# Attention and two MoE layers on one core: the MoE-only part without GpSimd, x staged by quarters, and fewer loader steps a turn

## The chip, the cores and the metric

The kernel runs on one core of a Trainium2 chip. The core has five engines with a queue of instructions each: TensorE (PE in the profile, its weight loads PEld), VectorE (DVE), ScalarE (ACT), GpSimd (POOL) and SyncE (SP, which here only issues DMAs). An engine takes its instructions strictly in the order of its queue; a semaphore makes one wait for another engine. The metric is device time in microseconds (us); lower is better.

## The reference

Attention with a threshold, then two feed-forward layers on its output:

```python
scores = scale * np.matmul(q, k.transpose(0, 1, 3, 2))        # 4 batches, 8 heads, 576 tokens, 64 wide
thresh = np.max(scores, axis=-1, keepdims=True) - tau
scores = np.where(scores >= thresh, scores, -1000000000.0)
attn = np.exp(scores - max); attn = attn / (sum + 1e-09); attn_out = np.matmul(attn, v)
x = attn_out as (2304 tokens, 512)
g = x @ w_gate; x = (g * sigmoid(g) * (x @ w_val)) @ w_out    # MoE 1: 512 -> 1536 -> 512
h = np.maximum(x @ w_in, 0.0); out = (h * h) @ w_out          # MoE 2: 512 -> 2048 -> 512
```

The weights are given in float64.

## The kernel before

Every product is made from operands that are split into a high part and a low part, three matmuls for one (high by high, high by low, low by high). So whatever TensorE reads has first to be split: a copy that gives the high part (on ScalarE, `ops.copy`, line 48) and a subtraction that gives the low part (`ops.sub`, line 56).

The program has two parts. Phase 1 (to line 850) is attention, with the first group of MoE 1 in its gaps. Phase 2 (from line 853) is MoE alone, and the change concerns it. It walks over seven groups of feed-forward tiles of 128 columns: group 0 (the last batch's share of MoE 1's first group, two blocks of 288 tokens, five tiles), groups 1 and 2 (the rest of MoE 1, three and four tiles) and groups 3 to 6 (MoE 2, four tiles each); from group 1 on a group has six blocks of 384 tokens. The names carry this: `k3_1_2_u` is group 3, block 1, tile 2.

A block is a step of `chain` (line 331). Its units come first, one for each tile: `gate_val` (two products of 12 matmuls each) or `relu2` (one product of 12). Line 218 is their matmul. What reads a product follows in stages (`mp.post`): for `relu2` ScalarE's Relu (L292), VectorE's square (L293), ScalarE's copy to the high part of `u`, VectorE's subtraction for its low part (L56, `k_u`). For `gate_val` they are a tanh (L238) and VectorE's L239 and L248, then the same copy and subtraction. The block's second product (`out1` L263, `out2` L309) reads the `u` of all its tiles. It is emitted two units into the next block (one in group 0), so those units cover the time that the last `u` takes.

Two more streams run beside this. First, x of the next block is split into `xs` (`stage_x`, line 167) in four chunks: ScalarE copies all four, GpSimd subtracts three and VectorE the fourth ("AAAA", "PPPD" on line 899). `xs` has two buffers. Second, the weights of the next group come in by pieces of 128x256 (`Loader`, line 97). A piece goes through a DMA into `wr` (L120), an absolute value on ScalarE (L129, into `wf`), four bit operations on VectorE (L131, L133, L137, L139, called the loader's first to fourth step below), a copy on ScalarE (the high part of `w`) and a subtraction on GpSimd (L56, the low part). `wr` and `wf` have three buffers, so a piece's DMA waits until the third piece before it is through L139. Lines 924 to 929 advance the loader after every three matmuls of a unit: a start, and up to one step on GpSimd, two on ScalarE and two on VectorE.

The framework sorts what was emitted by readiness and priority, so a queue need not keep the order of emission: loader steps move ahead to where their engine would be free. The queues shown below are the sorted ones.

Of the kernel before, what the change touches and what calls it, by code (L numbers as in the profile page):

```python
# [18 lines left out]
P = 128  # L19
# [16 lines left out]
# the upper word of float64 2**-127, read as a float32  # L36
# [26 lines left out]
def attention_moe(tc, qkv, qk0, tau, w1, w2, out, cfg):  # L63
# [14 lines left out]
    # MoE 1's output: the last batch's has a tile of its own, in phase 2  # L78
# [15 lines left out]
    # The weights come in as float64. A piece of a tile is brought to float32 from its bits: sign and  # L94
    # top exponent bit, the seven low exponent bits and the mantissa's first 23. What is too small for
    # float32 is raised to an exponent that gives 0 there. Then it is split.
    class Loader:
        """Brings the weights of f tiles in, piece by piece, each a little further at every call."""

        def __init__(self):  # L100
            self.bufs = []
            self.todo = []
            self.live = []
            self.n = 0
            self.age = 0

# [5 lines left out]
        def start(self):  # L112
            self.age += 1
            if not self.todo or sum(x[2] < 6 for x in self.live) >= LIVE:
                return
            src, f, w, c0 = self.todo.pop(0)
            self.n += 1
            sl = slice(c0, c0 + PIECE)
            raw, fl = self.bufs[self.n % LIVE]
            nc.sync.dma_start(raw, src[f, :, sl])  # L120
            g = self.steps(raw, fl, w[:, 0, sl], w[:, 1, sl], self.n)
            self.live.append([g, next(g), 1, "S", self.age, (f, c0)])

        def steps(self, raw, fl, whi, wlo, n):
# [17 lines left out]
            yield "P"  # L142
            ops.sub(cfg["wl"][self.n % 2], wlo, fl, whi.bitcast(F32))

        def tick(self, eng):
            """The next step on that engine, of the first piece that can take it."""
# [9 lines left out]
        def until(self, f, col):  # L156
            """Brings in what is left of tile f up to that column."""
            while any(x[1] == f and x[3] < col for x in self.todo) or any(
                x[5][0] == f and x[5][1] < col for x in self.live
            ):  # L160
                self.start()
                for e in "PADDDDP":
                    self.tick(e)
# [3 lines left out]
    def stage_x(src, xs, t0, n, eh, el):  # L167
        for c in range(NC):
# [4 lines left out]
    # split operands: hi*hi, hi*lo, lo*hi  # L173
    TERMS = [(c, a, b) for c in range(NC) for a, b in ((0, 0), (0, 1), (1, 0))]

    class Mm:
        """PSUM tiles of one bank each. What reads them is emitted in stages, later than the products."""
# [50 lines left out]
    # MoE 1, one f tile on one block: gate and value products, silu(gate) * value, split  # L228
# [100 lines left out]
    # Chains steps: a step's second product follows the next step's first unit, and what a step  # L329
    # needs first is made ready during the step before.  # L330
    def chain(steps, sync):
# [4 lines left out]
        def begin(i):  # L336
            if i < len(steps) and i not in begun:
                begun.add(i)
                steps[i]["begin"]()

        for i, s in enumerate(steps):
# [3 lines left out]
            us = []  # L345
            for j in range(s["G"]):
                u = None
                for u, c in s["unit"](j):
                    yield c
                us.append(u)  # L350
                if j == s.get("ahead", 0) and i + 1 < len(steps) and steps[i + 1].get("need") == s.get("need"):
                    begin(i + 1)
# [11 lines left out]
    # ======================= phase 1: attention, with MoE 1's first group in its gaps =======================  # L364
# [3 lines left out]
    # the last batch's part of xF is not written before the other batches are through: at first the loader has it  # L368
# [11 lines left out]
    # a column next to the scores passes every threshold and meets the 1e-9 that is added to the sum  # L380
# [5 lines left out]
    # half of the scores on either side of a bank's end  # L386
# [24 lines left out]
    def head(h):  # L411
        """The tiles of a head: queries' high and low parts one above the other, keys' twice, values' side by side."""
# [9 lines left out]
    # Where TensorE has time to spare (the first batch), products with the values may be in float32: then the  # L422
    # probabilities and the values stay whole. They lie in x2, which has nothing in it yet.
# [3 lines left out]
    def whole(p, i):  # L427
        """Is tile i of pair p (are all or some tiles of the pair) so treated?"""
# [22 lines left out]
    def first_pair():  # L451
        """Each head is loaded twice, one below the other, and split in both places."""
# [33 lines left out]
    def pair_steps(p):  # L486
        """A pair's queries and keys are split with one head above the other, then brought to their tiles by DMA."""
# [143 lines left out]
    def halves(t):  # L631
        """A tile's two PSUM tiles: the first slot of each, how many, and the way of its low parts."""
# [107 lines left out]
    def fill_group():  # L740
        """One whole product of MoE work; its PE columns, or None when there is none to do."""
# [19 lines left out]
    def work(i):  # L761
        """At most one product an iteration: attention's first, else MoE's."""
# [89 lines left out]
    # ======================= phase 2: MoE 1's other groups, then MoE 2 =======================  # L852
# [24 lines left out]
    wts[0] = W  # L877
    for _ in range(len(groups[1][2])):
        load_next(1)
# [6 lines left out]
    def steps2():  # L886
        for idx in range(len(groups)):
# [5 lines left out]
            for j, (t0, n) in enumerate(blocks):  # L893
# [3 lines left out]
                def begin(d=d, t0=t0, n=n, nm=nm, kind=kind):  # L897
                    xs = xs2.tile([P, 2, NC, n], F32R, name=f"xs_{nm}", tag="xs")
                    d["xs"] = stage_x([(0, xF)] if kind == 1 else x2, xs, t0, n, "AAAA", "PPPD")

                def end(idx=idx, j=j):
# [8 lines left out]
                    "begin": begin,  # L910
# [12 lines left out]

    for _ in chain(steps2(), mp2.drain):
        mp2.age += 1
        mp2.flush()
        loader.start()
        for e in "PADDA":
            loader.tick(e)
# [6 lines left out]
def pack(inputs):  # L936
# [37 lines left out]
# Engines: A ScalarE, D VectorE, P GpSimd. "early" and "early0" (first batch): how far ahead of its place in the  # L974
# program the scheduler may take a step.
# [13 lines left out]
    "wl": "PP",  # L989
# [36 lines left out]
```

## Time and profile before

| | |
|---|---|
| time, median of 3 runs | 1233.13 us (1233.12 to 1233.24) |
| span of the profiled execution | 1234.0 us; the page gives no other time of it |
| PE busy | 1177.9 us, 95% |
| DVE busy | 878.7 us, 71% |
| ACT busy | 654.1 us, 53% |
| POOL busy | 519.1 us, 42% |
| mean granted TensorE clock | 0.988 |

The profiled span is 0.9 us above the median. Phase 2's first matmul starts at 485.91 us, its last ends 3.8 us before the span's end; the rows below take that part apart. In a row of the timeline the first number is the start, the second how long the instruction lasted, and what stands in brackets is the idle time ahead of it and who ended it. Since instructions of one engine overlap at their ends, the time that one occupies its engine is the distance to the start of the next, where that one waits for nothing.

### The profile page before, as it was taken

How to read it: one execution, taken by the hardware profiler on the slowest of the kernel's cores; microseconds unless marked ns; L12 is line 12 of the kernel's file. 1: busy time of each engine (PE TensorE's matmuls, PEld its weight loads, DVE VectorE, ACT ScalarE, POOL GpSimd, SP SyncE). 2: the span in 40 equal slices, each digit the busy share in tenths (PEclk: the TensorE clock that was granted, in tenths of full speed). 3: DMA queues.
4: the chain of work that ended last, by engine and by line, in shares of the span. 5: the costliest groups of instructions: out<-in, count | busy, mean ns of one | idle time of the engine just before them, and what ended most of it. 6: DMA issues, size and time to landing. Idle time of an engine off the chain costs nothing.

```text
span 1234.0 us, 20272 instructions
## 1 busy us (share of the span) xinstructions
PE 1177.9 (95%) x7008; PEld 1083.3 (88%) x7008; DVE 878.7 (71%) x1911; ACT 654.1 (53%) x1622; POOL 519.1 (42%) x649
## 2 busy tenths in 40 slices
PE   5999988999999999899899999998998999899998
PEld 4655878999999999899899999997997999799997
DVE  6877997899898983979845953478349648844453
ACT  5777877888777873545323421255445434533231
POOL 4445865677666743435222321153135215421120
PEclk9999999999999999999899999998999999999999
DMA  5564453444333401323300300012002101100111
GB/s 168 146 183 122 125 136 79 102 112 115 89 89 89 117 2 35 112 77 96 93 2 26 110 2 1 1 50 88 1 6 93 40 1 50 37 1 1 52 49 54
DMA packets 40854, 84.80 MB, mean 69 GB/s; under 512 B 5936, under 2 KB 6960, under 8 KB 40752
## 3 DMA queue, kind: packets, MB, share of 16 engines
q1 hardware_dynamic: 40752, 83.52, 24.2%
q8 instruction: 55, 0.90, 0.3%
q14 instruction: 47, 0.39, 0.1%
HBM read 52.23 MB, written 4.72 MB: 46 GB/s over the span
## 4 chain that ended last, share of the span: by engine, by line
PE 69%; DVE 17%; issue 5%; ACT 3%; POOL 2%; DMA 2%; SPq 1%; DVEq 0%; POOLq 0%; ACTq 0%
PE mm L218 24%; PE mm L309 14%; PE mm L263 7%; PE s L561 5%; PE bank L218 5%; PE bank L621 5%; PE bank L263 4%; PE bank L680 3%; PE bank L677 3%; DVE wf L137 3%; DVE wf L139 2%; DVE wf L133 2%; DVE e L590 1%; DVE wf L131 1%; DVE k_u L56 1%
## 5 line engine op out<-in xcount | busy, mean ns | idle before, releaser
L218 PE MATMUL mm<-xs_k,w 128*128 128x384 f32 (+1 forms) x2400 | 413.2, 330 | 0.5 <-ACT x L48 0.5
L218 PEld LDWEIGHTS mm<-xs_k,w 128*128 128x128 f32 x2400 | 407.8, 188 | 2.5 <-ACT x L48 0.7
L309 PE MATMUL mm<-w,k_u 128*128 128x512 f32 x864 | 210.2, 400 | 13.8 <-ACT k_u L48 9.4
L309 PEld LDWEIGHTS mm<-w,k_u 128*128 128x128 f32 x864 | 165.0, 193 | 52.8 <-ACT k_u L48 11.7
L56 POOL TENSOR_TENSOR w<-wf,w 128x256 fp32r<-128x256 f32 x116 | 98.6, 858 | 180.4 <-ACT w L48 180.3
L621 PE MATMUL bank<-ident,e 128*128 128x128 f32 x720 | 163.4, 279 | 6.8 <-POOL e L601 2.7
L601 POOL TENSOR_SCALAR e<-e,r 128x576 f32<-128x576 f32 x144 | 114.2, 794 | 86.4 <-DVE r L596 37.4
L48 ACT ACTIVATE k_u<-k_th 128x384 fp32r<-128x384 f32 (+1 forms) x148 | 76.6, 518 | 137.6 <-DVE k_th L293 77.3
L56 POOL TENSOR_TENSOR xs_k<-x,xs_k 128x384 fp32r<-128x384 f32 (+1 forms) x60 | 66.5, 1128 | 181.2 <-ACT xs_k L48 180.1
L56 DVE TENSOR_TENSOR k_u<-k_th,k_u 128x384 fp32r<-128x384 f32 (+1 forms) x148 | 92.5, 625 | 68.3 <-ACT k_u L48 68.0
L218 PE MATMUL bank<-xs_m,w 128*128 128x288 f32 x720 | 136.8, 325 | 2.0 <-DVE xs_m L56 1.7
L590 DVE SCALAR_TENSOR_TENSOR e<-s,thr,e 128x577 f32<-128x577 f32 x144 | 117.0, 813 | 15.5 <-ACT thr L581 8.1
L621 PEld LDWEIGHTS bank<-ident,e 128*128 128x128 f32 x720 | 95.5, 141 | 29.4 <-issue 16.3
L573 DVE TENSOR_REDUCE nm<-s 128x1 f32<-128x576 f32 x144 | 108.4, 754 | 18.1 <-PE s L561 16.9
L263 PE MATMUL mm<-k_u,w 128*128 128x384 f32 (+1 forms) x624 | 111.1, 336 | 8.1 <-DVE k_u L56 4.3
L263 PEld LDWEIGHTS mm<-k_u,w 128*128 128x128 f32 x624 | 107.9, 195 | 9.4 <-DVE k_u L56 5.1
L579 ACT ACTIVATE e<-s,nm 128x576 f32<-128x576 f32 x144 | 107.4, 746 | 15.0 <-PE bank L621 8.5
L218 PEld LDWEIGHTS bank<-xs_m,w 128*128 128x128 f32 x720 | 111.2, 189 | 4.5 <-DVE xs_m L56 3.4
L641 ACT ACTIVATE pt<-bank 128x384 fp32r<-128x384 f32 (+1 forms) x216 | 92.0, 437 | 35.8 <-PE bank L621 31.6
L293 DVE TENSOR_TENSOR k_th<-k_th 128x384 f32<-128x384 f32 x96 | 69.0, 719 | 58.7 <-ACT k_th L292 58.6
L292 ACT ACTIVATE k_th<-mm 128x384 f32<-128x384 f32 x96 | 46.3, 483 | 112.4 <-PE mm L218 112.4
L680 PE MATMUL bank<-pt,vs 128*128 128x256 f32 (+1 forms) x480 | 93.0, 322 | 1.6 <-POOL pt L56 1.2
(92 smaller groups left out, 1846.7 us busy)
## 6 DMA issues: line engine op xcount, KB each, us to landing
wr<-in_w_dram SPq DMA_DIRECT2D x106, 256.0 KB, 3.1
raw<-in_qkv_dram SPq DMA_DIRECT2D x15, 896.0 KB, 4.8
kh<-land SPq DMA_DIRECT2D x60, 144.0 KB, 2.6
kl<-raw SPq DMA_DIRECT2D x60, 144.0 KB, 2.7
xF<-in_w_dram SPq DMA_DIRECT2D x30, 256.0 KB, 2.9
out_dram<-xF SPq DMA_DIRECT2D x18, 256.0 KB, 2.0
qs<-land SPq DMA_DIRECT2D x30, 144.0 KB, 2.4
qs<-raw SPq DMA_DIRECT2D x30, 144.0 KB, 2.6
```

The costliest lines, as they stand in the source:

```text
L48: nc.scalar.activation(out, in_, AF.Copy)
L56: e.tensor_tensor(out, a, b, op=ALU.subtract)
L218: mm(pt[:, :n], w[:, a, col + c * P : col + (c + 1) * P], xs[:, b, c, :], start=(i == 0), stop=(i == len(TERMS) - 1),)
L263: mm(pt[:, :n], w[:, a, 2 * DM + m * P : 2 * DM + (m + 1) * P], u[:, b, :], start=(k == 0), stop=(k == last),)
L309: mm(pt, u[:, b, s * P : (s + 1) * P], w[:, a, DM : 2 * DM], start=(k == 0), stop=(k == last),)
L573: nc.vector.tensor_reduce(nm, sv, axis=AX.X, op=ALU.max, negate=True)
L579: nc.scalar.activation(e[:, :S], st[t]["s"][:, :S], AF.Exp, bias=st[t]["nm"])
L590: nc.vector.scalar_tensor_tensor(e, st[t]["s"][:, : S + 1], st[t]["thr"], e, op0=ALU.is_ge, op1=ALU.mult, accum_out=sum_)
L601: nc.gpsimd.tensor_scalar(e, e, scalar1=r, scalar2=1.0, op0=ALU.mult, op1=ALU.mult)
L621: mm(dst[:, j], e[:, c0 : c0 + P], ident, is_transpose=True, start=(j == 0), stop=(j == len(cols) - 1),)
L641: nc.scalar.activation(pt[:, s0 : s0 + n, o : o + P], src, AF.Copy)
L680: mm(o[:, :n], hd["vs"][:, SLOT[k % 5], :], pt[:, k, lo : lo + n], start=(k == 0), stop=(k == 9))
```

## The change

In phase 2 the subtractions for `xs` and for the weights go from GpSimd to VectorE. `chain` begins the next block's x by quarters, one after every fourth yield of a unit (three matmuls a yield), in place of all four after the first unit. The loader starts a piece only at every second turn and only while fewer than two pieces (three before) are short of their fourth step; a turn ticks ScalarE once, VectorE once, and VectorE a second time at every fourth turn. Phase 1 keeps its settings. Lines in the changed kernel stand 14 to 15 further down (L56 and L48 stay). Comments that the change takes out are left out here.

```diff
-            if not self.todo or sum(x[2] < 6 for x in self.live) >= LIVE:
+            if not self.todo or sum(x[2] < 6 for x in self.live) >= cfg["live"][self.phase]:
...
             ops.copy("A", whi, fl)
-            yield "P"
-            ops.sub(cfg["wl"][self.n % 2], wlo, fl, whi.bitcast(F32))
+            yield cfg["wl"][self.phase]
+            ops.sub(cfg["wl"][self.phase], wlo, fl, whi.bitcast(F32))
...
+            for c in range(NC) if part is None else (part,):
+                if (i, c) not in begun:
+                    begun.add((i, c))
+                    steps[i]["begin_part"](c)
...
                 for u, c in s["unit"](j):
                     yield c
+                    y += 1
+                    if "begin_part" in s and y % 4 == 0 and y // 4 <= NC:
+                        begin(i + 1, y // 4 - 1)
...
-                    d["xs"] = stage_x([(0, xF)] if kind == 1 else x2, xs, t0, n, "AAAA", "PPPD")
+                    stage_x([(0, xF)] if kind == 1 else x2, d["xs"], t0, n, "AAAA", "DDDD", (c,))
...
+    turn = 0
     for _ in chain(steps2(), mp2.drain):
         mp2.age += 1
         mp2.flush()
-        loader.start()
-        for e in "PADDA":
-            loader.tick(e)
+        turn += 1
+        if turn % 2:
+            loader.start()
+        loader.tick("A")
+        loader.tick("D")
+        if turn % 4 == 0:
+            loader.tick("D")
...
-    "wl": "PP",
+    "wl": "PD",
+    "live": (3, 2),
```

The queues of TensorE and SyncE keep their order from end to end. On VectorE and ScalarE the first difference comes at the end of phase 1, and on GpSimd too.

VectorE in group 0 (block 0, from tile 1's L239 or L240 on), before:

```order
L239 SCALAR_TENSOR_TENSOR k0_0_1_th_6538<-k0_0_1_th_6538,mm2_6459 128x288
L139 SCALAR_TENSOR_TENSOR wf20_6436<-wr0_6435,wf20_6436 128x256
L56 TENSOR_TENSOR k0_0_0_u_6475<-k0_0_0_th_6474,k0_0_0_u_6475 128x288
L131 TENSOR_SCALAR wf21_6438<-wf21_6438 128x256
L248 SCALAR_TENSOR_TENSOR k0_0_1_th_6538<-k0_0_1_th_6538,mm3_6460 128x288
L133 TENSOR_SCALAR wf21_6438<-wf21_6438 128x256
L137 SCALAR_TENSOR_TENSOR wf21_6438<-wr1_6437,wf21_6438 128x256
L56 TENSOR_TENSOR k0_0_1_u_6539<-k0_0_1_th_6538,k0_0_1_u_6539 128x288
```

The same place in the changed kernel, up to tile 2's first row:

```order
L240 SCALAR_TENSOR_TENSOR k0_0_1_th_6517<-k0_0_1_th_6517,mm2_6459 128x288
L134 TENSOR_SCALAR wf20_6436<-wf20_6436 128x256
L56 TENSOR_TENSOR w1536_5_6441<-wf22_6440,w1536_5_6441 128x256
L249 SCALAR_TENSOR_TENSOR k0_0_1_th_6517<-k0_0_1_th_6517,mm3_6460 128x288
L138 SCALAR_TENSOR_TENSOR wf20_6436<-wr0_6435,wf20_6436 128x256
L132 TENSOR_SCALAR wf21_6438<-wf21_6438 128x256
L140 SCALAR_TENSOR_TENSOR wf20_6436<-wr0_6435,wf20_6436 128x256
L56 TENSOR_TENSOR k0_0_1_u_6518<-k0_0_1_th_6517,k0_0_1_u_6518 128x288
L134 TENSOR_SCALAR wf21_6438<-wf21_6438 128x256
L56 TENSOR_TENSOR w1536_5_6441<-wf20_6436,w1536_5_6441 128x256
L138 SCALAR_TENSOR_TENSOR wf21_6438<-wr1_6437,wf21_6438 128x256
L240 SCALAR_TENSOR_TENSOR k0_0_2_th_6567<-k0_0_2_th_6567,mm4_6461 128x288
```

The weights' subtractions (L56 into `w1536`) now stand between a tile's rows.

VectorE in group 3, from block 1's tile 2 to its tile 3, before:

```order
L293 TENSOR_TENSOR k3_1_2_th_9537<-k3_1_2_th_9537 128x384
L139 SCALAR_TENSOR_TENSOR wf22_6440<-wr2_6439,wf22_6440 128x256
L131 TENSOR_SCALAR wf20_6436<-wf20_6436 128x256
L56 TENSOR_TENSOR k3_1_2_u_9538<-k3_1_2_th_9537,k3_1_2_u_9538 128x384
L133 TENSOR_SCALAR wf20_6436<-wf20_6436 128x256
L131 TENSOR_SCALAR wf21_6438<-wf21_6438 128x256
L137 SCALAR_TENSOR_TENSOR wf20_6436<-wr0_6435,wf20_6436 128x256
L293 TENSOR_TENSOR k3_1_3_th_9552<-k3_1_3_th_9552 128x384
L139 SCALAR_TENSOR_TENSOR wf20_6436<-wr0_6435,wf20_6436 128x256
L133 TENSOR_SCALAR wf21_6438<-wf21_6438 128x256
L137 SCALAR_TENSOR_TENSOR wf21_6438<-wr1_6437,wf21_6438 128x256
L56 TENSOR_TENSOR k3_1_3_u_9553<-k3_1_3_th_9552,k3_1_3_u_9553 128x384
```

The same place in the changed kernel:

```order
L294 TENSOR_TENSOR k3_1_2_th_9533<-k3_1_2_th_9533 128x384
L132 TENSOR_SCALAR wf22_6440<-wf22_6440 128x256
L56 TENSOR_TENSOR w1024_6_9881<-wf21_6438,w1024_6_9881 128x256
L134 TENSOR_SCALAR wf22_6440<-wf22_6440 128x256
L56 TENSOR_TENSOR k3_1_2_u_9534<-k3_1_2_th_9533,k3_1_2_u_9534 128x384
L138 SCALAR_TENSOR_TENSOR wf22_6440<-wr2_6439,wf22_6440 128x256
L132 TENSOR_SCALAR wf20_6436<-wf20_6436 128x256
L294 TENSOR_TENSOR k3_1_3_th_9550<-k3_1_3_th_9550 128x384
L56 TENSOR_TENSOR xs_k3_3_9592<-x2_65,xs_k3_3_9592 128x384 x2
L56 TENSOR_TENSOR k3_1_3_u_9551<-k3_1_3_th_9550,k3_1_3_u_9551 128x384
L56 TENSOR_TENSOR xs_k3_3_9592<-x2_65,xs_k3_3_9592 128x384
```

Two chunks of block 3's x now stand ahead of block 1's last `u`. Ahead of the first row shown, back to `k3_1_1_u`, stand 21 loader rows before (five each of L131, L133 and L139, six of L137) and 27 in the changed kernel (five each of the first two steps, six each of the last two, and five subtractions).

GpSimd at the same place in group 3, before:

```order
L56 TENSOR_TENSOR xs_k3_2_9468<-x2_65,xs_k3_2_9468 128x384 x3
L56 TENSOR_TENSOR w1024_5_9723<-wf22_6440,w1024_5_9723 128x256
L56 TENSOR_TENSOR w1024_5_9723<-wf20_6436,w1024_5_9723 128x256
L56 TENSOR_TENSOR w1024_6_9884<-wf21_6438,w1024_6_9884 128x256
L56 TENSOR_TENSOR w1024_6_9884<-wf22_6440,w1024_6_9884 128x256
```

And the last rows that GpSimd has in the changed kernel, which belong to phase 1:

```order
L56 TENSOR_TENSOR m21_2_u_6263<-m21_2_th_6262,m21_2_u_6263 128x288
L52 TENSOR_SCALAR m21_3_u_6294<-m21_3_th_6293 128x288
L56 TENSOR_TENSOR m21_3_u_6294<-m21_3_th_6293,m21_3_u_6294 128x288
L52 TENSOR_SCALAR m21_4_u_6326<-m21_4_th_6325 128x288
L56 TENSOR_TENSOR m21_4_u_6326<-m21_4_th_6325,m21_4_u_6326 128x288
```

All that GpSimd did behind them is on VectorE: 106 subtractions for weights, and for x 96 of 128x384, 24 of 128x192 and 6 of 128x288.

## Rows read from the trace of the kernel before

**Rows 1.** Stretches: phase 2 whole (length, then busy time and count by engine).
```profile
485.91:1234.00 748.09, 722.44 (x3888) 679.85 (x3888) 474.73 (x922) 292.87 (x694) 220.51 (x226) 0.98 0.14 44
```
**Rows 2.** What TensorE waited for in phase 2: us in total, times, longest.
```profile
PE mm L309 <- ACT k_u L48: 9.4, 5, 3.2
...
PE mm L309 <- DVE k_u L56: 4.2, 3, 3.0
```
**Rows 3.** Stretches, each one second product: length, PE, PEld, DVE, ACT, POOL, clock, DMA.
```profile
505.21:519.07 13.86, 10.00 (x62) 9.55 (x61) 12.59 (x27) 6.27 (x17) 7.18 (x8) 0.88 0.33 98
540.20:548.16 7.96, 7.96 (x62) 7.96 (x61) 2.72 (x6) 3.51 (x9) 0.48 (x1) 1.00 0.00 0
...
598.80:612.12 13.32, 9.48 (x37) 8.90 (x37) 12.44 (x27) 5.85 (x15) 4.99 (x5) 0.74 0.31 98
624.60:630.84 6.24, 6.24 (x37) 6.24 (x37) 2.69 (x5) 0.53 (x1) 0.00 (x0) 1.00 0.01 1
838.75:855.41 16.66, 11.75 (x37) 8.46 (x37) 15.72 (x34) 9.46 (x23) 6.81 (x7) 0.80 0.28 84
863.76:871.96 8.20, 8.20 (x38) 6.76 (x37) 2.68 (x5) 2.22 (x4) 1.24 (x2) 1.00 0.00 0
...
947.04:962.48 15.44, 11.15 (x38) 7.80 (x37) 14.93 (x31) 8.55 (x21) 7.01 (x7) 0.78 0.23 74
1053.56:1068.59 15.03, 10.68 (x37) 7.43 (x37) 14.04 (x27) 8.13 (x20) 7.15 (x8) 0.89 0.12 40
```
**Rows 4.** Timeline of VectorE around group 3's block 1 (start, duration).
```profile
826.09 0.55 DVE L293 TENSOR_TENSOR k_th<-k_th 128x384 f32<-128x384 f32 x1
826.56 0.42 DVE L137 SCALAR_TENSOR_TENSOR wf<-wr,wf 128x256 int32<-128x256 int32 x1
826.89 0.28 DVE L133 TENSOR_SCALAR wf<-wf 128x256 int32<-128x256 int32 x1
827.10 0.42 DVE L139 SCALAR_TENSOR_TENSOR wf<-wr,wf 128x256 int32<-128x256 int32 x1
827.43 0.55 DVE L56 TENSOR_TENSOR k_u<-k_th,k_u 128x384 fp32r<-128x384 f32 x1
827.90 0.42 DVE L137 SCALAR_TENSOR_TENSOR wf<-wr,wf 128x256 int32<-128x256 int32 x1
...
839.26 0.55 DVE L293 TENSOR_TENSOR k_th<-k_th 128x384 f32<-128x384 f32 x1
...
842.62 1.22 DVE L139 SCALAR_TENSOR_TENSOR wf<-wr,wf 128x256 int32<-128x256 int32 x1
843.76 1.08 DVE L133 TENSOR_SCALAR wf<-wf 128x256 int32<-128x256 int32 x1
...
858.24 0.56 DVE L293 TENSOR_TENSOR k_th<-k_th 128x384 f32<-128x384 f32 x1 [1.71 <-ACT k_th L292]
859.39 0.56 DVE L56 TENSOR_TENSOR k_u<-k_th,k_u 128x384 fp32r<-128x384 f32 x1 [0.59 <-ACT k_u L48]
```
**Rows 5.** Timeline of GpSimd in the same stretch.
```profile
842.25 3.45 POOL L56 TENSOR_TENSOR xs_k<-x,xs_k 128x384 fp32r<-128x384 f32 x3
```
**Rows 6.** GpSimd's groups in phase 2, the two largest (busy us, mean ns).
```profile
L56 POOL TENSOR_TENSOR w<-wf,w 128x256 fp32r<-128x256 f32 x106 | 90.9, 866 | 171.3 <-ACT w L48 171.3
L56 POOL TENSOR_TENSOR xs_k<-x,xs_k 128x384 fp32r<-128x384 f32 x48 | 57.2, 1217 | 147.5 <-ACT xs_k L48 146.4 <-POOL w L56 1.0
```
**Rows 7.** Timeline of VectorE at the start of group 0.
```profile
488.31 0.46 DVE L239 SCALAR_TENSOR_TENSOR k_th<-k_th,mm 128x288 f32<-128x288 f32 x1 [10.86 <-ACT k_th L238]
...
490.12 0.42 DVE L139 SCALAR_TENSOR_TENSOR wf<-wr,wf 128x256 int32<-128x256 int32 x1
...
494.94 0.45 DVE L248 SCALAR_TENSOR_TENSOR k_th<-k_th,mm 128x288 f32<-128x288 f32 x1
495.30 0.68 DVE L133 TENSOR_SCALAR wf<-wf 128x256 int32<-128x256 int32 x1
```
**Rows 8.** Timeline of ScalarE in the same stretch.
```profile
494.26 0.43 ACT L129 ACTIVATE wf<-wr 128x256 f32<-128x256 f32 x1 [1.06 <-DMA wr<-in_w_dram]
```

More of the change, by code (lines that the diff above doesn't have):

```diff
@@ L105, in __init__ @@
             self.age = 0
+            self.phase = 0
         def add(self, src, f, width, pool):
@@ L165, in attention_moe, with stage_x @@
     loader = Loader()
-    def stage_x(src, xs, t0, n, eh, el):
-        for c in range(NC):
+    def stage_x(src, xs, t0, n, eh, el, chunks=range(NC)):
+        for c in chunks:
             for x, a, o, w in parts(src, t0, n):
@@ L334, in chain, with begin @@
         begun = set()
[L336 to L339, printed above, removed]
+        def begin(i, part=None):
+            if i >= len(steps):
+                return
+            if "begin" in steps[i]:
+                if i not in begun:
+                    begun.add(i)
+                    steps[i]["begin"]()
+                return
+            for c in range(NC) if part is None else (part,):
+                if (i, c) not in begun:
+                    begun.add((i, c))
+                    steps[i]["begin_part"](c)
         for i, s in enumerate(steps):
@@ L345, in chain @@
             us = []
+            y = 0
             for j in range(s["G"]):
@@ L349, in chain @@
                     yield c
+                    y += 1
+                    if "begin_part" in s and y % 4 == 0 and y // 4 <= NC:
+                        begin(i + 1, y // 4 - 1)
                 us.append(u)
-                if j == s.get("ahead", 0) and i + 1 < len(steps) and steps[i + 1].get("need") == s.get("need"):
+                if "begin" in s and j == s.get("ahead", 0) and i + 1 < len(steps) and steps[i + 1].get("need") == s.get("need"):
                     begin(i + 1)
@@ L877, in attention_moe @@
     wts[0] = W
+    loader.phase = 1
     for _ in range(len(groups[1][2])):
@@ L895, in steps2, with begin_part @@
                 d = {}
-                def begin(d=d, t0=t0, n=n, nm=nm, kind=kind):
-                    xs = xs2.tile([P, 2, NC, n], F32R, name=f"xs_{nm}", tag="xs")
-                    d["xs"] = stage_x([(0, xF)] if kind == 1 else x2, xs, t0, n, "AAAA", "PPPD")
+                def begin_part(c, d=d, t0=t0, n=n, nm=nm, kind=kind):
+                    if "xs" not in d:
+                        d["xs"] = xs2.tile([P, 2, NC, n], F32R, name=f"xs_{nm}", tag="xs")
+                    stage_x([(0, xF)] if kind == 1 else x2, d["xs"], t0, n, "AAAA", "DDDD", (c,))
                 def end(idx=idx, j=j):
@@ L909, in steps2 @@
                     "lag": int(len(fs) < 5),
-                    "begin": begin,
+                    "begin_part": begin_part,
                     "unit": lambda q_, d=d, n=n, nm=nm, idx=idx, unit=unit: unit(
```

## The prediction

> **What bounds the kernel now.** I read the page first, then phase 2 by stretches, then TensorE's waits, then the timelines of the engines that it waits for. On the page the reader sees a TensorE that is busy 95% of the span; so only its idle time and its clock can be won. Phase 1 keeps its queues, so I look at phase 2 alone: 748.09 us, of which TensorE works 722.44, VectorE 474.73 and GpSimd 220.51 [rows 1].
>
> The list of waits says what the idle time is: `out2` (L309) waits for ScalarE's copy and VectorE's subtraction of `k_u`, 9.4 and 4.2 us, in a handful of instances of up to 3 us [rows 2]. So I cut phase 2 at the second products and compare each with an undisturbed one of its kind [rows 3]. In group 0 one takes 13.86 us where its twin takes 7.96; in group 1 one 13.32 against 6.24; in MoE 2 three take 16.66, 15.44 and 15.03 against 8.20. The excess is 5.90 + 7.08 + 8.46 + 7.24 + 6.83 = 35.5 us. Length less busy time gives the idle part: 3.86 + 3.84 + 4.91 + 4.29 + 4.35 = 21.3 us. The other 14.3 us is the clock: its mean is 0.74 to 0.89 in these five and 1.00 in the twins, so after each wait the matmuls ran for some us at the lower of the two levels, 1.2 in place of 2.4 GHz. A microsecond of such waiting therefore costs 35.5 / 21.3 = 1.7 us.
>
> In all five VectorE is busy 91 to 97% of the time, while GpSimd is busy too; in the twins VectorE has 2.7 us to do [rows 3]. The timeline shows why `u` is late [rows 4, 5]. With GpSimd idle a 384-wide square or subtraction occupies VectorE for 0.47 us (826.09 to 826.56, 827.43 to 827.90), a loader step of two inputs 0.33, of one input 0.21. Under GpSimd's three x subtractions (842.25, 3.45 us) an L139 takes 1.22 where it took 0.42, an L133 1.08 where it took 0.28. And `u` stands behind many of these in the queue.
>
> **What is taken from VectorE and what is added.** Added: 106 weight subtractions at 0.33 (two inputs of 256, as L137 and L139 [rows 4]) = 35 us; 96 x subtractions of 384 at 0.47 = 45; 24 of 192 at about 0.25 and 6 of 288 at 0.36 (494.94 to 495.30 [rows 7]) = 8. Together 88 us, for which GpSimd spent 220.5 (0.87 for a weight's, 1.22 for a full x chunk [rows 6]). What contention costs VectorE is not a row, so I bound it: nothing at all, or all that its rows last beyond the uncontended ones. Spread over the whole of phase 2 even the first bound, (474.7 + 88) / 748, is 75%: no limit by itself. What decides is the queue in front of each late `u`, so I count rows there.
>
> **Group 3, block 1 (the 16.66 us product).** Units of `relu2` take (863.76 - 855.41) / 4 = 2.09 us [rows 3]. Call T the end of tile 1's unit: 838.75 - 8.35 - 8.20 = 822.20. Undisturbed, a square starts 0.74 us after its unit's end (855.41 + 2.09 = 857.50 to 858.24) and the subtraction 1.15 after that [rows 4]; so tile 1's `u` is done at T + 0.74 + 1.15 + 0.47 = T + 2.4, and its loader rows fit into the 1.15. Then come 27 loader rows in the changed queue, 10 at 0.21 and 17 at 0.33 = 7.7 us. The 21 rows before make 5.7 by the same prices, and took 839.26 - 827.90 = 11.36 [rows 4]: 5.6 us more. That is partly contention, which goes, and partly the loader's own turn, which stays: in three buffers the next piece can only start when the DMA has refilled `wr`. From the time that L139 frees VectorE (490.12 + 0.33) to the end of the next absolute value in the same buffer (494.26 + 0.43 [rows 7, 8]) are 4.2 us. In the changed queue 2.1 to 3.2 us of rows stand between a piece's last step and its buffer's next first one, so about 3 us of waits remain in the 27 rows: 10.7 us. Ends: 7.7 (no wait) and 13.3 (the whole 5.6 stays). Tile 2's square is thus reached at T + 13.1, 2.0 after it could run (T + 8.20 + 2.09 + 0.74). From there to the end of tile 3's `u` stand two squares, two `u`, two x chunks and five loader rows, 4.1 us: T + 17.2. TensorE needs that low part at the product's eleventh matmul, T + 8.20 + 8.35 + 10 x 0.228 = T + 18.8. Spare: 1.6 us, against a wait of 4.9 before; at the upper end it would be 1.0 us late.
>
> **Group 0.** Here `out1` follows after one unit, so the cover is thin. From tile 0's first row to tile 4's `u` the changed queue has 15 rows of 288 at 0.36, 19 loader rows at 0.21 and 26 at 0.33: 18.0 us. Begun at 488.31 [rows 7], it ends at 506.3; TensorE needs tile 4's low part at the fourteenth matmul, 505.21 + 13 x 0.133 = 506.9 [rows 3]. The rows between a buffer's pieces make 3.4 to 4.1 us against the turn of 4.2, and following these shortfalls down the queue adds 0 to 2.5 us, which I take at 1.6: 1.0 us late, x 1.7 = 1.7 us lost in place of 5.9.
>
> **The other three.** Group 1's blocks have an 18.7 us period (three times its 6.24) with 17 rows of 0.47, 8 us, and about six pieces a block at 1.4: 16.4 us, so they keep up, and a `gate_val` unit gives four us of cover. The places in groups 4 and 5 resemble the one in group 3, with two or three fewer rows between the tiles. I set 0.5 us for what of these I did not follow.
>
> **Edits costed at nothing.** Taking x by quarters moves no TensorE row. A block's `xs` can be written only when its buffer's last reader is through, a whole block (16.5 us) ahead of need, and both queues show it written there; the cover would be gone if it came in the last two units. But two chunks now stand ahead of the last `u` (0.94 us, counted above). In a block without a loader the `u` is needed 2 x 2.09 + 10 x 0.228 = 6.5 us after its unit and done after 0.74 + 0.47 + 0.94 + 0.47, with a gap some 2.7: hidden, 3.7 to spare. Fewer pieces in flight let weights land later, yet they are wanted only in the next group; the burst in group 3 ends with its block 2, three blocks ahead. SyncE's queue keeps its order, and its DMAs have no other user than the output. ScalarE does what it did.
>
> **Sum.** 1234.0 - 35.5 + 1.7 + 0.5 = 1200.7 for the profiled execution; the median lay 0.9 below it: **1199.8 us**, 2.7% less. Its own range is 1195 to 1206: no wait left and some of the small ones gone too, or 1 to 2 us late at each of the five.
>
> **Rivals.**
> First, VectorE stays the bound. For it: it is 91 to 97% busy in the five places, and its queue there grows from 21 to 27 rows. If each row keeps the mean of before, 11.36 / 21 = 0.54, the 27 take 14.6 us, tile 3's `u` ends at T + 21.1, 2.3 us late where it was 4.9. With half the waits half the loss stays: 1199.8 + 17 = **1216**. Against: rows of the same kind ran at 0.21 and 0.33 wherever GpSimd was idle. The Trainium skill speaks for this rival (Perfetto Trace Analysis, Optimizing Scalar/DVE Operations): where VectorE is saturated, giving work to GpSimd may pay, and here the change takes it back. The same section warns that the two share a port, so that such a shift might not help; rows 4 and 5 bear the warning out.
>
> Second, the pacing does not happen. The sorting still puts 27 loader rows between two tiles, so "one step a product" is not what the queue shows. If the turn of the buffers is what made the five waits, it makes them again: some 5 us gained from shorter rows, **1228**. Against: of the wait's causes it explains 3 of 5.6 us.
>
> Third, slower: x in front of `u`. In every one of MoE 2's 24 blocks the last `u` now waits for two chunks, hence for ScalarE's two copies and for the release of `xs`. It decides from a delay of 3.7 us on; 2 us beyond that in each block, without any change of clock, would be 48 us: **1247**. For: the order shows it in block after block. Against: the copies run when VectorE's square runs, and 3.7 us is eight such rows.
>
> **Chances.** Forecast 0.70, first rival 0.18, second 0.06, third 0.06. The range 1194 to 1218 takes in the forecast's own and the first rival's, 0.85 or so. A difference under 0.2% (2.5 us) could not be told from none here. Faster: 0.70 + 0.18 + half of the second = 0.91; same 0.03; slower 0.06.
>
> **What would show it.** Right: L131 and L133 at 0.28 everywhere, L293 and `k_u` at 0.55; no GpSimd row in phase 2; second products of MoE 2 at 8.20 all through with a clock of 1.00; a short wait, if any, in group 0. Wrong in size: waits of 1 to 3 us at the second products under loading, with VectorE's rows short but its idle time ahead of L131 up. Wrong in kind: `k_u` late in blocks where no weights come in, or matmuls of L218 waiting for `xs`.

## The result and the profile after

| | before | after |
|---|---|---|
| time, median | 1233.18 us (1233.12 to 1234.86) | 1199.74 us (1198.72 to 1200.79), 4 runs |
| span of the profiled execution | 1234.0 us | 1196.9 us |
| phase 2, from its first matmul to the span's end | 748.09 us | 713.15 us |

The ratio is 0.9723, 95% interval 0.9709 to 0.9737: 2.8% faster, where 2.7% was predicted (1199.8 us). Phase 2 gave 34.9 us in the two profiles; the other 2.2 us is phase 1, whose end lies between 483.6 and 487.1 us in the profiles here of kernels that leave GpSimd nothing more to do there, and which the change can't be credited with.

The first rows of the page of after: busy time, share and instructions of each engine, then GpSimd's and the clock's 40 slices.

```profile
PE 1162.6 (97%) x7008; PEld 1074.8 (90%) x7008; DVE 868.2 (73%) x2143; ACT 652.1 (54%) x1622; POOL 293.8 (25%) x417
...
POOL 4445875676776663000000000000000000000000
PEclk9999998999999999999999999999999999999999
```

GpSimd stops at the end of phase 1. VectorE, which took over 226 subtractions, is busy for less time than before (868.2 against 878.7 us in the whole span). Next the windows of after: length, busy time (and instructions) of PE, PEld, DVE, ACT and POOL, clock, DMA share, GB/s. The first is phase 2; the others are second products: group 0's and group 1's, then those of MoE 2 that answer to the three long ones, and the one that starts at 939.87.

```profile
483.75:1196.90 713.15, 708.54 (x3888) 672.15 (x3888) 462.41 (x1148) 290.87 (x694) 0.00 (x0) 1.00 0.15 46
503.05:512.13 9.08, 8.51 (x62) 8.06 (x61) 8.44 (x28) 5.44 (x15) 0.00 (x0) 1.00 0.42 130
591.17:597.41 6.24, 6.24 (x37) 6.24 (x37) 5.82 (x18) 2.01 (x5) 0.00 (x0) 1.00 0.36 118
824.04:832.24 8.20, 8.20 (x38) 6.76 (x37) 7.54 (x22) 5.30 (x13) 0.00 (x0) 1.00 0.18 57
923.32:931.52 8.20, 8.20 (x38) 6.76 (x37) 7.85 (x22) 4.37 (x12) 0.00 (x0) 1.00 0.14 49
939.87:948.75 8.88, 8.63 (x38) 6.60 (x38) 7.24 (x19) 4.81 (x15) 0.00 (x0) 1.00 0.13 39
1023.28:1031.48 8.20, 8.20 (x38) 6.76 (x37) 7.81 (x23) 4.15 (x11) 0.00 (x0) 1.00 0.14 47
```

Against [rows 1]: length less TensorE's busy time was 25.7 us and is 4.6 (3.8 of it behind the last matmul, as before), so 21.0 us of idle time went. The same 3888 matmuls take 13.9 us less, and the mean clock of the phase went from 0.98 to 1.00. The five long products of [rows 3] are gone: group 1's takes 6.24 us, the three of MoE 2 take 8.20, and only group 0's is still long, 9.08 for the 7.96 of its twin. The one at 939.87, the next after a long one of before and undisturbed there, now lasts 8.88. TensorE's waits in phase 2 of after say the same (us in total, times, longest), against the 9.4 and 4.2 us of [rows 2]:

```profile
PE mm L219 <- ACT x L48: 0.5, 1, 0.5
PE mm L264 <- DVE k_u L56: 0.4, 1, 0.4
PE mm L310 <- DVE k_u L56: 0.3, 1, 0.3
PE mm L264 <- ACT k_u L48: 0.2, 1, 0.2
```

VectorE's groups in phase 2 of after (busy us, mean ns of one; idle time ahead and who ended it):

```profile
L56 DVE TENSOR_TENSOR k_u<-k_th,k_u 128x384 fp32r<-128x384 f32 x138 | 76.7, 556 | 47.6 <-ACT k_u L48 47.2
L294 DVE TENSOR_TENSOR k_th<-k_th 128x384 f32<-128x384 f32 x96 | 53.3, 555 | 52.4 <-ACT k_th L293 52.1
...
L134 DVE TENSOR_SCALAR wf<-wf 128x256 int32<-128x256 int32 x106 | 30.3, 288 | 0.6
...
L249 DVE SCALAR_TENSOR_TENSOR k_th<-k_th,mm 128x384 f32<-128x384 f32 x42 | 23.2, 551 | 18.8 <-PE mm L219 18.6
```

The same `u` and the loader's second step in phase 2 of before:

```profile
L56 DVE TENSOR_TENSOR k_u<-k_th,k_u 128x384 fp32r<-128x384 f32 x138 | 88.0, 638 | 67.8 <-ACT k_u L48 67.5
...
L133 DVE TENSOR_SCALAR wf<-wf 128x256 int32<-128x256 int32 x106 | 43.9, 416 | 1.4
```

Each mean of after is the uncontended length: 0.556 us for `u` (0.638 before), 0.288 for the loader's second step (0.416 before, 1.08 where [rows 4] shows it under GpSimd's work). The last row of after is one that reads a product from PSUM.

### The profile page after: what moved, and what is told of

It reads as the page before. It is cut to its first block, busy times and chain, and to the rows that moved or that the text cites. A ratio compares the mean times of both kernels' runs of the same rounds, so it can differ in the third digit from the quotient of the medians.

```text
span 1196.9 us, 20191 instructions
## 1 busy us (share of the span) xinstructions
PE 1162.6 (97%) x7008; PEld 1074.8 (90%) x7008; DVE 868.2 (73%) x2143; ACT 652.1 (54%) x1622; POOL 293.8 (25%) x417
## 4 chain that ended last, share of the span: by engine, by line
PE 79%; DVE 9%; DMA 3%; ACT 3%; issue 2%; POOL 2%; SPq 1%; POOLq 0%; DVEq 0%; ACTq 0%
PE mm L219 30%; PE mm L310 15%; PE mm L264 9%; PE s L575 5%; PE bank L635 5%; PE bank L219 4%; PE bank L264 4%; PE bank L694 4%; PE bank L691 3%; DMA wr<-in_w_dram 2%; DVE e L604 2%; DVE nm L587 1%; POOL e L615 1%; DMA raw<-in_qkv_dram 1%; DVE xs_k L56 1%
## 5 line engine op out<-in xcount | busy, mean ns | idle before, releaser
L310 PE MATMUL mm<-w,k_u 128*128 128x512 f32 x864 | 201.3, 391 | 0.3 <-DVE k_u L56 0.3
L310 PEld LDWEIGHTS mm<-w,k_u 128*128 128x128 f32 x864 | 161.5, 188 | 34.0 <-DVE k_u L56 1.0
L48 ACT ACTIVATE k_u<-k_th 128x384 fp32r<-128x384 f32 (+1 forms) x148 | 76.3, 516 | 90.0 <-DVE k_th L294 47.0
L56 DVE TENSOR_TENSOR k_u<-k_th,k_u 128x384 fp32r<-128x384 f32 (+1 forms) x148 | 81.2, 549 | 47.8 <-ACT k_u L48 47.4
L593 ACT ACTIVATE e<-s,nm 128x576 f32<-128x576 f32 x144 | 107.4, 746 | 14.3 <-PE bank L635 7.0
L264 PE MATMUL mm<-k_u,w 128*128 128x384 f32 (+1 forms) x624 | 106.1, 327 | 0.6 <-DVE k_u L56 0.4
L264 PEld LDWEIGHTS mm<-k_u,w 128*128 128x128 f32 x624 | 103.7, 188 | 1.0 <-DVE k_u L56 0.6
L575 PE MATMUL s<-kh,qs 128*128 128x288 f32 x256 | 78.1, 319 | 14.2 <-DVE qs L484 7.2
L294 DVE TENSOR_TENSOR k_th<-k_th 128x384 f32<-128x384 f32 x96 | 53.3, 555 | 52.4 <-ACT k_th L293 52.1
L48 ACT ACTIVATE w<-wf 128x256 fp32r<-128x256 f32 x116 | 46.8, 413 | 57.0 <-DVE wf L140 43.3
```

The costliest lines, as they stand in the source:

```text
L48: nc.scalar.activation(out, in_, AF.Copy)
L56: e.tensor_tensor(out, a, b, op=ALU.subtract)
L264: mm(pt[:, :n], w[:, a, 2 * DM + m * P : 2 * DM + (m + 1) * P], u[:, b, :], start=(k == 0), stop=(k == last),)
L310: mm(pt, u[:, b, s * P : (s + 1) * P], w[:, a, DM : 2 * DM], start=(k == 0), stop=(k == last),)
L575: mm(sp[:, cols], l, r[:, cols], start=(n_ == 0), stop=(n_ == len(pairs) - 1),)
L593: nc.scalar.activation(e[:, :S], st[t]["s"][:, :S], AF.Exp, bias=st[t]["nm"])
```

## The experiments

Theory A: GpSimd's work lengthens VectorE's rows, so the last `u` comes late; the subtractions' move is the whole gain. Theory B: it is the new pace of the loader, or x by quarters. Phase 2 of each profile, by length and busy time of TensorE alone, besides the medians (before, run again beside them, was 1235.33 us with e1 to e4, 1233.67 with e5 to e9, 1233.5 with e10 and e11):

| | median us | ratio to before, 95% | phase 2 us | PE idle | PE busy |
|---|---|---|---|---|---|
| before | | | 748.09 | 25.7 | 722.44 |
| after | 1199.74 | 0.9723 (0.9709 to 0.9737) | 713.15 | 4.6 | 708.54 |
| e1_x_on_dve | 1206.68 | 0.9768 (0.9751 to 0.9785) | 718.06 | 8.0 | 710.10 |
| e2_w_on_dve | 1209.07 | 0.9795 (0.9775 to 0.9815) | 724.13 | 11.6 | 712.54 |
| e3_both_on_dve | 1199.31 | 0.9711 (0.9695 to 0.9727) | 713.61 | 5.2 | 708.40 |
| e4_pace_only | 1233.13 | 0.9982 (0.9969 to 0.9995) | 746.93 | 25.1 | 721.87 |
| e5_old_pace | 1201.54 | 0.9737 (0.9715 to 0.9759) | 714.07 | 5.4 | 708.67 |
| e7_idle_gpsimd | 1228.17 | 0.9952 (0.9938 to 0.9966) | 734.24 | 17.5 | 716.78 |
| e8_idle_copy | 1216.20 | 0.9856 (0.9838 to 0.9874) | 721.70 | 9.1 | 712.56 |
| e9_group0 | 1197.89 | 0.9711 (0.9696 to 0.9726) | 711.80 | 3.9 | 707.87 |
| e10_after_again | 1201.85 | 0.9733 (0.9713 to 0.9752) | 712.55 | 4.4 | 708.17 |
| e11_group0_again | 1199.47 | 0.9717 (0.9697 to 0.9737) | 712.24 | 4.1 | 708.12 |

### x alone on VectorE (e1)

Before, with one word changed; x is begun whole and the loader keeps its pace (`...` marks what is left out).

```diff
-  stage_x(..., xs, t0, n, "AAAA", "PPPD")
+  stage_x(..., xs, t0, n, "AAAA", "DDDD")
```

> The kernel before with one edit: VectorE makes all four x subtractions, GpSimd keeps the weights' subtractions; old pace, x at once. Theory A (GpSimd's work lengthens VectorE's rows, so the last u is late): GpSimd's 130 us of x go, its 91 us of weights stay and fall in the loaded stretches, so about half the loss goes: 1212 to 1222 us, waits of 1 to 2 us in each of the five second products. Theory B (the pace and the order of the loader's rows make u late): the order of the loader's rows is nearly that of before, so the five waits stay: 1228 to 1235 us.

Measured: 718.06 us for phase 2, 30.0 of the 34.9 us. The median, 1206.68, lies below theory A's range (1212 to 1222) and far from B's: the move of x does more than half. TensorE's waits for `u` and two groups of VectorE of this kernel:

```profile
PE mm L309 <- ACT k_u L48: 2.7, 3, 1.7
PE mm L263 <- DVE k_u L56: 0.9, 1, 0.9
```

```profile
L56 DVE TENSOR_TENSOR k_u<-k_th,k_u 128x384 fp32r<-128x384 f32 x138 | 77.8, 564 | 46.8 <-ACT k_u L48 46.5
...
L133 DVE TENSOR_SCALAR wf<-wf 128x256 int32<-128x256 int32 x106 | 42.3, 404 | 1.1
```

GpSimd still has the weights' subtractions, and the loader's steps, which run beside them, are still long (L133 404 ns, 288 in after), while `u` is nearly at its short length.

### Weights alone on VectorE (e2)

```diff
-            yield "P"
-            ops.sub(cfg["wl"][self.n % 2], wlo, fl, whi.bitcast(F32))
+            yield cfg["wl"][self.phase]
+            ops.sub(cfg["wl"][self.phase], wlo, fl, whi.bitcast(F32))
...
-        for e in "PADDA":
+        for e in "DADDA":
...
-    "wl": "PP",
+    "wl": "PD",
```

> The kernel before with one edit: VectorE makes the weights' subtractions, GpSimd keeps three of the four x subtractions; old pace, x at once. Theory A: the x subtractions still meet VectorE's rows just as u is made, with 6 more loader rows in front of a late u, so most waits stay: 1215 to 1235 us. Theory B: the pace is as before, 1228 to 1240 us.

Measured: 724.13 us, 24.0 of the 34.9. The median, 1209.07, is again below theory A's range (1215 to 1235). The mirror of e1, in the largest waits and in groups:

```profile
PE mm L310 <- DVE k_u L56: 4.9, 3, 2.1
PE mm L264 <- DVE k_u L56: 2.4, 1, 2.4
```

```profile
L56 DVE TENSOR_TENSOR k_u<-k_th,k_u 128x384 fp32r<-128x384 f32 x138 | 89.0, 645 | 67.4 <-ACT k_u L48 67.0
...
L134 DVE TENSOR_SCALAR wf<-wf 128x256 int32<-128x256 int32 x106 | 32.7, 313 | 0.7
```

Now L134 is nearly short, while `u` stays long (645 ns): it is what runs when x is staged. 30.0 and 24.0 add up to 54, not to 34.9. This fits waits that begin only where the delays in one queue exceed its spare, so that either half alone takes most of them away; both expectations had set the halves too low.

### Both on VectorE, old pace, x at once (e3)

Before with the edits of e1 and e2 together.

> The kernel before with GpSimd's work in phase 2 on VectorE, and nothing else: old pace, x at once. Theory A: all of the gain, 1198 to 1204 us, with short waits in group 0 only. Theory B: without the new pace the five waits stay, 1222 us or more.

Measured: the whole gain. Phase 2 is 713.61 us against 713.15 in after, the median 1199.31. TensorE's waits for `u` come to 1.3 us in all, the longest 0.7, all of them at `out1`. The group of `u`:

```profile
L56 DVE TENSOR_TENSOR k_u<-k_th,k_u 128x384 fp32r<-128x384 f32 x138 | 76.5, 555 | 47.6 <-ACT k_u L48 46.9
```

So A holds, and for the pace and the quarters together there is nothing left to explain that can be told from the scatter.

### Pace and quarters alone (e4)

After, with GpSimd's work given back.

```diff
-  stage_x(..., d["xs"], t0, n, "AAAA", "DDDD", (c,))
+  stage_x(..., d["xs"], t0, n, "AAAA", "PPPD", (c,))
+        loader.tick("P")
-    "wl": "PD",
+    "wl": "PP",
```

> The changed kernel with GpSimd's work given back to GpSimd: the new pace and x by quarters alone. Theory A: hardly a gain, 1225 to 1235 us, L133 and its kind again over 0.35 us in the mean. Theory B: most of the gain, 1198 to 1210 us.

Measured: 0.2% faster, 746.93 us of phase 2 with 25.1 us of idle time where before had 25.7. The waits of [rows 2] (9.4 and 4.2 us) and the long rows of before (638 and 416 ns) are all there, with the loader's new pace and x by quarters:

```profile
PE mm L310 <- ACT k_u L48: 10.2, 5, 3.2
...
PE mm L310 <- DVE k_u L56: 3.4, 3, 1.7
```

```profile
L56 DVE TENSOR_TENSOR k_u<-k_th,k_u 128x384 fp32r<-128x384 f32 x138 | 87.4, 634 | 67.0 <-ACT k_u L48 66.7
...
L134 DVE TENSOR_SCALAR wf<-wf 128x256 int32<-128x256 int32 x106 | 44.2, 419 | 1.5
```

### The old pace in after (e5)

```diff
-        if turn % 2:
-            loader.start()
-        loader.tick("A")
-        loader.tick("D")
-        if turn % 4 == 0:
-            loader.tick("D")
+        loader.start()
+        for e in "DADDA":
+            loader.tick(e)
...
-    "live": (3, 2),
+    "live": (3, 3),
```

> The changed kernel with the old pace (three pieces in flight, a start and up to three VectorE steps at every turn), GpSimd idle, x by quarters. Theory A: as the changed kernel, phase 2 of 712 to 716 us, a wait of about 1 us in group 0. Theory B: 720 us or more, waits of 1 us and more at three or more second products.

Measured: 714.07 us of phase 2, 0.9 more than after, and a median of 1201.54, between after's own two (1199.74 and 1201.85 in e10). So the pace is worth a microsecond or so, if anything. Since e3 differs from e5 only in beginning x at once, the quarters are worth nothing that can be told either.

### GpSimd busy with work that nobody waits for (e7)

The runs above change VectorE's queue together with GpSimd's work. This one separates them: after, with two more subtractions on GpSimd behind each staged chunk of x, into a tile that nobody reads. The order of the other four engines is that of after, row for row, and no engine waits for GpSimd in phase 2.

```diff
+    dz = p2.enter_context(tc.tile_pool(name="dz", bufs=1)).tile([P, 192], F32, name="dz")
...
+                    for _ in range(2):
+                        ops.sub("P", dz, d["xs"][:, 0, c, :192].bitcast(F32), d["xs"][:, 1, c, :192].bitcast(F32))
```

> The changed kernel plus work on GpSimd that nobody waits for: after each staged chunk of x two subtractions of 128x192 from xs into a scratch tile, eight a block, some 6 us a block or 200 us in phase 2, about what GpSimd did before. The queues of the four other engines keep the changed kernel's order row for row. Theory A (VectorE's rows are lengthened while GpSimd works): L134 and k_u longer in the mean, waits of TensorE for k_u are back in the loaded blocks, phase 2 longer than the changed kernel's 713 us by 5 to 30 us. Theory C (what cost time before was waiting for GpSimd's results and the row order that came of it, not the overlap): nothing changes, 713 us within 1.

Measured: phase 2 at 734.24 us, 21.1 more than after, with 12.9 us more idle time and 8.2 us more busy time for the same matmuls. The median rose by 28.4 us and the profiled span by 30.7; the other 9.6 of that lie at the end of phase 1 (phase 2 starts at 493.36 us), where the added rows stand ahead of phase 1's own on GpSimd. GpSimd's row, TensorE's waits, and the groups of VectorE, all in phase 2:

```profile
L56 POOL TENSOR_TENSOR dz<-xs_k 128x192 f32<-128x192 f32 x288 | 223.8, 777 | 482.1 <-DVE xs_k L56 461.0 <-ACT x2b L48 2.2
```

```profile
PE mm L310 <- ACT k_u L48: 7.6, 8, 1.6
PE mm L310 <- DVE k_u L56: 4.8, 6, 1.2
```

```profile
L56 DVE TENSOR_TENSOR k_u<-k_th,k_u 128x384 fp32r<-128x384 f32 x138 | 100.4, 727 | 43.6 <-ACT k_u L48 43.3
L294 DVE TENSOR_TENSOR k_th<-k_th 128x384 f32<-128x384 f32 x96 | 71.2, 742 | 44.7 <-ACT k_th L293 44.6
...
L134 DVE TENSOR_SCALAR wf<-wf 128x256 int32<-128x256 int32 x106 | 34.4, 327 | 0.6
...
L249 DVE SCALAR_TENSOR_TENSOR k_th<-k_th,mm 128x384 f32<-128x384 f32 x42 | 23.1, 550 | 15.0 <-PE mm L219 14.1
```

GpSimd's 223.8 us are about the 220.5 of before, though not at the same places: here they follow x, so `u` and the squares are hit and L134 less. One such place in the timeline, VectorE and then GpSimd (start, us, what; idle time ahead in brackets):

```profile
904.34 0.56 DVE L56 TENSOR_TENSOR k_u<-k_th,k_u 128x384 fp32r<-128x384 f32 x1 [0.59 <-ACT k_u L48]
905.27 0.56 DVE L294 TENSOR_TENSOR k_th<-k_th 128x384 f32<-128x384 f32 x1 [0.37 <-ACT k_th L293]
...
909.31 0.95 DVE L294 TENSOR_TENSOR k_th<-k_th 128x384 f32<-128x384 f32 x1
910.85 0.97 DVE L56 TENSOR_TENSOR k_u<-k_th,k_u 128x384 fp32r<-128x384 f32 x1 [0.59 <-ACT k_u L48]
```

```profile
906.44 6.72 POOL L56 TENSOR_TENSOR dz<-xs_k 128x192 f32<-128x192 f32 x8 [9.84 <-DVE xs_k L56]
```

From 906.44 on the same two instructions last 0.95 and 0.97 us in place of 0.56. That is the mechanism by itself: nothing but work on GpSimd was added. What in the hardware the two engines share, no run here shows.

### The same with copies (e8)

Four passes of one tensor by constants (L52) in place of two subtractions, so 576 rows of 0.45 us.

```diff
-                    for _ in range(2):
-                        ops.sub("P", dz, d["xs"][:, 0, c, :192].bitcast(F32), d["xs"][:, 1, c, :192].bitcast(F32))
+                    for _ in range(4):
+                        ops.copy("P", dz, d["xs"][:, 1, c, :192].bitcast(F32))
```

> As the run with idle subtractions, but with four copies of 128x192 (one input from SBUF each) after each chunk in place of two subtractions. If what counts is only that GpSimd is busy, VectorE's rows lengthen as much for each us of GpSimd; if two inputs are what collides, they lengthen less and phase 2 stays within 3 us of 713.

Measured: phase 2 at 721.70 us, 8.5 more than after. GpSimd is busy longer than in e7 and does less harm:

```profile
L52 POOL TENSOR_SCALAR dz<-xs_k 128x192 f32<-128x192 f32 x576 | 260.7, 453 | 435.0 <-DVE xs_k L56 390.6
```

```profile
L56 DVE TENSOR_TENSOR k_u<-k_th,k_u 128x384 fp32r<-128x384 f32 x138 | 84.6, 613 | 44.1 <-ACT k_u L48 44.0
```

So what counts is not GpSimd's busy time as such: per microsecond of it, rows with two tensor inputs cost phase 2 0.094 us (21.1 / 223.8), those with one 0.033 (8.5 / 260.7). Since part of a delay is hidden in the spare, VectorE's own busy time is the more direct measure: it rose from 462.41 us in after to 545.22 in e7 and 501.18 in e8, 0.37 and 0.15 us for each microsecond. The expectation had set at most 3 us for the copies, so one input does less harm but not none. The two kinds of row also differ in length and number, which these runs do not separate.

### A slower loader in group 0 (e9, e10, e11)

What is left of the five waits stands in group 0, where tile 4's `u` is the 60th row of VectorE from tile 0's first on. This is after with one piece in flight for the first 48 turns:

```diff
+        cfg["live"] = (3, 1 if turn <= cfg["slow"] else 2)
...
+    "slow": 48,
```

> The changed kernel with one piece in flight in the first 48 turns, that is up to group 0's first second product, where the changed kernel still loses 1.1 us. VectorE's queue has 48 rows in place of 60 up to tile 4's u. If the rows in front of that u are what makes it late, the wait there goes and phase 2 is 1.1 us shorter, 712 us; if the turn of the loader's buffers is, it stays. Time 1197 to 1201 us.

The wait is gone (that `u` is the 48th row in place of the 60th). TensorE in this kernel, with no gap in the 60 matmuls, which now take 7.98 us:

```profile
503.60 8.14 PE L264 MATMUL mm<-k_u,w 128*128 128x288 f32 x60
511.58 1.62 PE L219 MATMUL mm<-xs_k,w 128*128 128x288 f32 x11
```

Phase 2 took 711.80 us, 1.35 less. The medians of e9 and after come from different sets of runs, so both ran again side by side.

> The changed kernel once more, beside the next one on one chip: 1198 to 1201 us, phase 2 of 713 us.

> The version with one piece in flight until group 0's first second product, on the same chip: phase 2 of 712 us, 1.3 us shorter than the changed kernel's; in the median between 0 and 2.5 us shorter, since phase 1 scatters by 2 us or so.

Again e11 is ahead: 1199.47 against 1201.85 us, with ratios 0.9717 (0.9697 to 0.9737) and 0.9733 (0.9713 to 0.9752), which overlap. In phase 2 it is 712.24 against 712.55. So the wait is shown to go, while the time it saves (0.3 us in this pair of profiles, 1.35 in the first, where 1.3 was expected) is too small to tell in the total: no version here can be told to be faster than after.

Not tried: more buffers for `wr` and `wf`, which would shorten the waits for the loader's turn.

## Why the prediction was right

**The loss and its two parts.** It held that 35.5 us at five second products were all to be won, 21.3 idle and 14.3 of clock. 21.0 us of idle time and 13.9 of busy time went. Some 1.8 us stay in group 0 and at 939.87 (1.12 + 0.68 us more than undisturbed), where 2.2 were set (1.7 + 0.5), and 34.9 - 35.5 + 1.8 = 1.2 us came from two more second products of before, which I had not counted: those at 579.40 and 929.94 took 6.92 and 8.76 us, 0.68 and 0.56 more than undisturbed, and in after they take 6.24 and 8.20.

The clock's part of the loss was set too high. In before the granted clock of phase 2 was at the lower level (0.50) in five stretches, one in each long product, from 511.22, 603.38, 845.73, 951.54 and 1060.77 on. Their lengths together, and TensorE's busy time in them:

```profile
sum 27.32, PE 22.63; mean PE 4.53
```

At the higher level this work would take half as long, so the clock cost 11.3 us by this estimate, and not 14.3. The other 3.0 us is longer busy time that came with the waits at the full clock; what it is stays open. In phase 2 of after no stretch has the lower clock. The sum needed only both parts together, so the forecast did not suffer. E7 shows the price of 1.7 us for a microsecond of such waiting from the other side: 12.9 us of idle time came with 21.1 in all, 1.6 to 1. Of its 8.2 us of busy time the clock makes up 4.4 by the same estimate (8.70 us busy at the lower level). No run tried the clock by itself.

**The bound on contention.** Of the two ends, nothing or all that VectorE's rows last beyond the uncontended ones, the second was taken, and e3, e4 and e7 show it. VectorE's busy time in phase 2 even fell with 226 subtractions more (474.73 to 462.41 us); with the 88 us that the prediction put on them, contention had cost VectorE some 474.73 + 88 - 462.41 = 100 us, an estimate.

**Group 3, block 1.** This is where its working can be followed row by row. VectorE in after, from tile 1's `u` through the loader's rows to tile 2's square, and on to tile 3's `u`:

```profile
809.58 0.55 DVE L56 TENSOR_TENSOR k_u<-k_th,k_u 128x384 fp32r<-128x384 f32 x1
810.05 0.42 DVE L138 SCALAR_TENSOR_TENSOR wf<-wr,wf 128x256 int32<-128x256 int32 x1
...
816.81 0.29 DVE L132 TENSOR_SCALAR wf<-wf 128x256 f32<-128x256 f32 x1 [0.53 <-ACT wf L130]
...
820.36 0.55 DVE L294 TENSOR_TENSOR k_th<-k_th 128x384 f32<-128x384 f32 x1
...
825.05 0.55 DVE L56 TENSOR_TENSOR k_u<-k_th,k_u 128x384 fp32r<-128x384 f32 x1
```

The 27 rows took 820.36 - 810.05 = 10.3 us; predicted were 10.7 between ends of 7.7 and 13.3. The waits for the loader's turn that were to stay are there: 10.3 - 7.7 = 2.6 us where 3 were set, the longest of them in the bracket shown. With T = 824.04 - 8.20 - 8.35 = 807.49, tile 2's square came at T + 12.9 (predicted 13.1). But tile 3's `u` was done at 825.05 + 0.47, which is T + 18.0 and not T + 17.2, so the spare was 0.8 us and not 1.6. The reason stands on ScalarE:

```profile
822.79 0.43 ACT L130 ACTIVATE wf<-wr 128x256 f32<-128x256 f32 x1 [1.07 <-DMA wr<-in_w_dram]
823.13 0.47 ACT L293 ACTIVATE k_th<-mm 128x384 f32<-128x384 f32 x1
```

An absolute value that waits 1.07 us for its DMA stands ahead of tile 3's Relu, and ScalarE takes its queue in order (tile 3's unit had ended at T + 8.20 + 2 x 2.09 = 819.87). I had looked at VectorE's queue alone and put ScalarE at nothing ("ScalarE does what it did"); its waits for the loader's DMA grew (30.0 to 47.3 us in phase 2), and this one ate half the spare. The 0.25 us at 939.87 shows the same in a block where the spare did not suffice. There tile 2's unit ended at 931.52 + 2.09 = 933.6, and its Relu came at 938.31, behind this row:

```profile
937.98 0.43 ACT L130 ACTIVATE wf<-wr 128x256 f32<-128x256 f32 x1 [2.00 <-DMA wr<-in_w_dram]
```

**Group 0.** Predicted were 19.6 us for the queue (18.0 and 1.6 of waits); it took from 486.15 to 505.65, 19.5. TensorE needed that low part at 503.05 + 13 x 0.133 = 504.78, so it came 0.9 us late, where 1.0 was set. The wait shows in two parts of 0.18 and 0.39 us, and the product lasted 1.1 us longer in place of 1.7:

```profile
505.00 0.40 PE L264 MATMUL mm<-k_u,w 128*128 128x288 f32 x1 [0.18 <-ACT k_u L48]
505.78 6.51 PE L264 MATMUL mm<-k_u,w 128*128 128x288 f32 x47 [0.39 <-DVE k_u L56]
```

For each microsecond of idle time this is 1.12 / 0.57 = 2.0 us, and at 939.87 0.68 / 0.25 = 2.7, both above the 1.7 that I had. But the extra 0.55 and 0.43 us of busy time can't be read as the lower clock: the column says 1.00 in both windows. What they are is open; e9 shows only that they go with the wait.

**The sum.** 1199.8 against 1199.74 is closer than its terms deserve, and that is luck. For the span 1200.7 us was forecast and 1196.9 came, 3.8 less: 1.6 in phase 2 (34.9 us gained where 35.5 - 2.2 = 33.3 were set) and 2.2 in phase 1, which scatters by as much or more. The 0.9 us taken off from the profiled span to the median was no offset between the two: the runs of after and of e9 to e11 are each 1.7 to 2.1 us above their own span, so this term had the wrong sign and was off by 2.7 us. The profiled run of after was also its fastest, 1.0 us below the median. 3.8 - 2.7 - 1.0 leaves the 0.1.

**The rivals.** VectorE as the bound (1216) would have left the 27 rows at a mean of 0.54 us; they took 10.3 / 27 = 0.38 each, waits included. For this rival stood the Trainium skill's advice that giving work to GpSimd may make sense where VectorE is saturated (Perfetto Trace Analysis, Optimizing Scalar/DVE Operations). Here the opposite paid, as e3 shows (748.09 to 713.61 us). The same section of the Trainium skill warns that this might not help, since the two share a port; e7 agrees with the warning (713.15 to 734.24 us), though no run shows that the port is the cause. The pace's not happening (1228) was half true: the sorting does undo it, but e5 and e4 show that it does not matter. The slower one (1247), x in front of `u`, fell: TensorE's waits for `u` are 0.9 us in all of phase 2 of after, and between e3, e5 and after, of which e3 begins x whole, phase 2 differs by 0.9 us at most.

## What to carry to other kernels

Before work is shared out between VectorE and GpSimd, compare the same instruction's length with the other engine idle and busy: here VectorE did 226 subtractions more in less busy time once GpSimd was still. What counts is the queue in front of the one late instruction, so follow each engine that feeds it, in the order of its queue, and not the mean load. To prove contention, add work that nobody waits for to the suspected engine, while the other queues stay row for row.

## What the runs showed of the hardware

- VectorE's rows that read a product from PSUM are not lengthened by GpSimd: L249's group is at 551 ns in after and 550 in e7, while squares go from 555 to 742. In e7 14 of the 42 rows of L249 ran wholly beside GpSimd's rows, at 548 ns in the mean. The rows that were lengthened have SBUF inputs alone.
- GpSimd's passes with one tensor input disturbed VectorE less than those with two, though they kept GpSimd busy longer (e7 and e8 above).
- ScalarE's waits for the loader's DMA rose with little harm to the total: L130 waits 47.3 us in phase 2 of after, 30.0 in before, and of this the trace shows 0.8 us of lost spare and the one late `u` above.
- A short wait of TensorE can cost more than itself without a fall of the granted clock: in after 0.57 and 0.25 us of idle time came with products 1.12 and 0.68 us longer, at a clock of 1.00.
